# Chunk-selected attention and a SwiGLU layer on one core: two neighbouring query blocks of the selection turned by one transpose

## The chip, the cores and the metric

The kernel runs on one core of a Trainium2 chip. The metric is device time in microseconds (us), the median of several runs. A core has a matrix engine (TensorE, PE in the profile), a vector engine (DVE), a scalar engine (ACT), a general engine (POOL) and a queue engine (SP); each works through its own queue in order, and they meet through semaphores. Matmul results land in PSUM, eight banks of 2 KiB per partition; everything else is in SBUF.

## What is computed

Attention with 4 batches, 8 heads, 768 positions and head size 64, in which each query sees only 6 of 24 chunks of keys, chosen by an upper bound of its scores; then RMS normalisation and a SwiGLU layer (512 to 1536 and back) over the 3072 rows.

```python
k_chunks = k.reshape(B, H, nc, 32, D)
k_min, k_max = np.min(k_chunks, axis=3), np.max(k_chunks, axis=3)
ub = np.sum(np.maximum(q * k_min, q * k_max), axis=-1)      # per query and chunk
ub = np.where(causal, ub, -1e9)
top_chunks = np.argsort(ub, axis=-1)[..., -6:]
scores = scale * q @ k.T, masked to the chosen chunks and to keys not later than the query
attn = softmax(scores) @ v
x = attn rows of all heads side by side
g, val = rmsnorm(x) @ w_gate, rmsnorm(x) @ w_val
out = (silu(g) * val) @ w_out
```

## The kernel before, in words

The work goes by pairs of heads: 16 pairs (4 batches with 4 pairs each). For a pair, `prep` (line 471) loads q and k (SP queue), turns them with TensorE (line 499) so that 128 partitions hold two heads of 64 dimensions, and evicts them to SBUF (`kt`, `qt`). DVE reduces the keys of each chunk to minimum and maximum (lines 523, 525), POOL casts keys and queries to bf16 into the tiles `KE` and `QS` (line 319), and TensorE forms the bounds (line 578, six query groups side by side). The bounds are evicted (`ubs`), turned back so that queries are on partitions (`up`, line 602), and DVE adds the causal term (`ubm`, line 610), takes the eight largest of 24 (`max`, lines 621 to 623, 12 instructions per pair) and writes the selection (`pick`, lines 631 and 636): per query block and head 24 flags and one guard value.

The selection then has to stand on partitions again, beside the queries. `SELQ` holds for each of six query blocks of 128 queries a row of 2 heads x 64 columns, of which 25 are used. `sel_turn` (line 647) turns the six blocks with six transposes of 128x128 into one PSUM tile `st`, 64 partitions per head. `sel_out` (line 655) evicts one half per head into the free half of `QS`: for the first head (hl = 0) queries are in partitions 0 to 63 and flags in 64 to 127, for the second head the other way round. `KE` holds the keys in the same halves, and beside them the indicator rows `e_all`: row c is -30000 in the columns of chunk c, so that one matmul gives score plus mask. `scores` (line 687) runs these matmuls (line 712) over `kk` rows: 89 (64 + 25) for the first head and 128 for the second; for batch 0 a triangular mask is added by a further matmul (line 718), for the others POOL masks after exp (line 735). ACT does exp (line 729), TensorE multiplies by v (line 748), DVE divides (lines 763, 764). `norm` (line 776) and `ffn` (line 844) then work on half batches of 384 rows: 12 tiles of gate and value matmuls (lines 864, 885) with tanh on ACT and two products on DVE (lines 871, 877, 893), and the projection (line 905).

The constants are made at the start: the flags' tile is zeroed by DVE (line 358), `e_all` is built by POOL in four steps (lines 363 to 381) and copied into `KE` by DVE for the first of three buffers and by SP's DMA for the others (lines 387 to 396). `cmf` (line 398) is the causal term.

The order of all instructions is the result of a planner (`Order`, line 107). Each step has engines that it may run on, a cost, dependencies, buffers, and a rank: the sum of entries of two tables, `RANK` (by kind of step, one table for batch 0 and one for the others) and `TIMES` (by place: `a7` is the preparation of pair 7, `l7` its loads, `s7.0` its scores, `n1.0` and `f1.0` normalisation and feed-forward of a half batch, and `step`, `pace...` the increments within a place). The planner simulates the engines with its own costs, takes among the steps that are ready the one of least rank, and emits the instructions in that order. It charges `selC`, the two evictions of the selection, to DVE or ACT, whichever is free, and lets both run at once. The scores of a pair depend on all its `selC` steps in the plan; on the chip an instruction waits only for the tiles that it reads.

Of the kernel before, what the change touches and what calls it, by code (L numbers as in the profile page):

```python
# [8 lines left out]
FP32 = mybir.dt.float32  # L9
BF16 = mybir.dt.bfloat16  # L10
ALU = mybir.AluOpType
ACT = mybir.ActivationFunctionType
# [3 lines left out]
BIGE = 30000.0  # L16
BIGC = 1.0e30
BIGT = -30000.0
THRFLOOR = -5.0e29


GUARD = 480.0
# [5 lines left out]
        av=-17.99, dif=13.38, eps=15.18, exp=27.56, kC=-0.16, kE=17.53, kT=-23.78, kload=11.87,  # L28
        kmn=22.63, kmx=-12.26, max=-61.12, qC=54.11, qE=9.45, qT=-26.18, qload=3.56,
        relu=19.97, root=46.9, sc=-0.2, sel=-44.38, selC=-65.79, selT=-14.62, sq=17.6, tp=7.31,  # L30
        tpE=23.87, ub=-8.14, ubE=18.31, ubm=-7.93, up=-18.76, vload=-10.11, xb=16.97, xs=25.31,
    ),
    dict(
        av=-15.37, dif=-18.4, eps=-17.61, exp=10.72, gate=-5.25, hh=-22.22, kC=13.17, kE=-4.98,
        kT=-1.03, kload=0.17, kmn=-41.84, kmx=7.41, mask=-29.68, max=20.31, out=-9.4, po=2.14,
        poE=-2.1, qC=3.39, qE=-3.84, qT=-9.81, qload=-3.16, relu=-0.35, root=5.16, sc=-14.52,
        sel=-54.35, selC=-24.54, selT=7.81, sq=37.75, tanh=-21.52, tg=-0.17, tp=-45.38,
        tpE=12.9, ub=-13.71, ubE=24.1, ubm=13.82, up=-10.31, val=1.94, vload=19.85, xb=5.4,
        xs=11.14,
# [3 lines left out]
TIMES = dict(  # L43
    pace0=1.79, pace1=0.05, pacen=0.06, step=0.1, w=-2.85, w0=-2.54, w1=11.0, w2=43.12,
    w3=21.59,
)
for p, x in enumerate((
    13.52, 22.61, 22.24, 36.48, 50.85, 112.1, 73.87, -93.04, 37.77, 179.84, 214.26, 206.91,
    226.56, 220.49, 246.48, 309.33,
)):  # L50
    TIMES[f"a{p}"] = x
for p, x in enumerate((
    -126.16, -42.1, -31.16, -25.49, -5.8, -2.4, 25.7, 37.05, 124.03, 155.87, 181.98, 170.69,
    131.44, 202.23, 282.06, 292.24,
)):
    TIMES[f"l{p}"] = x
for p, x in enumerate((
    -21.19, 10.14, 25.24, 47.31, 25.73, 45.99, 41.69, 141.19, 75.77, 129.26, 185.37, 166.25,
    277.81, 251.34, 143.95, 194.34,
)):  # L60
    TIMES[f"s{p}.0"] = x
for p, x in enumerate((
    101.79,
), 3):
    TIMES[f"s{p}.3"] = x
for i, x in enumerate((
    -27.88, 91.19, 93.6, 105.43, 90.44, 106.14, 282.0, 341.37,
)):
    TIMES[f"n{i // 2}.{i % 2}"] = x
for i, x in enumerate((  # L70
    50.8, 120.12, 121.42, 191.74, 229.9, 291.93, 266.48, 339.66,
)):
    TIMES[f"f{i // 2}.{i % 2}"] = x
for i, x in enumerate((
    2.53, 0.58, 0.91, 2.16, 0.75, 2.5, 0.51, 0.73,
)):
    TIMES[f"pacef{i // 2}.{i % 2}"] = x

# [145 lines left out]
def kernel(  # L224
# [23 lines left out]
    HB = NT // 2  # L248
    KM = D + NCH + 1
    W = S // 2  # L250
    G = 3
# [76 lines left out]
    NB = SLOTS["set"]  # L328
# [8 lines left out]
    cmf = const.tile([P, NT, 2, NCH], FP32, name="cmf")  # L337
# [9 lines left out]
    def make_ident(e):  # L347
# [13 lines left out]
        VX[i][:, :, D:D + 1], 1.0)) for i in range(SLOTS["vext"])]  # L361

    def e_step(n):
        if n == 0:
            nc.gpsimd.memset(e_all[:], -BIGE)
        elif n == 1:
            nc.gpsimd.affine_select(
                out=e_all[:], in_=e_all[:], compare_op=ALU.is_ge, fill=0.0,
                base=0, pattern=[[1, S]], channel_multiplier=-CH,
            )  # L370
        elif n == 2:
            nc.gpsimd.affine_select(
                out=e_all[:], in_=e_all[:], compare_op=ALU.is_ge, fill=0.0,
                base=CH - 1, pattern=[[-1, S]], channel_multiplier=CH,
            )
        else:

            nc.gpsimd.affine_select(
                out=e_all[:], in_=e_all[:], compare_op=ALU.not_equal, fill=-1.0,
                base=-NCH, pattern=[[0, S]], channel_multiplier=1,  # L380
            )
# [4 lines left out]
    c_e = prev  # L386
# [11 lines left out]
    def make_cmf(n):  # L398
        if n == 0:
            nc.gpsimd.memset(cmf[:], 0.0)  # L400
        for g4 in (2 * n, 2 * n + 1):
            nc.gpsimd.affine_select(
                out=cmf[32 * g4:32 * (g4 + 1)], in_=cmf[32 * g4:32 * (g4 + 1)],
                compare_op=ALU.is_ge, fill=-BIGC,
                base=g4, pattern=[[4, NT], [0, 2], [-1, NCH]], channel_multiplier=0,
            )

    c_cm = add("cmf", "POOL", 1.5, -70, lambda e: make_cmf(0), [c_e])
# [62 lines left out]
    def prep(c, i0, nb, at, lr):  # L471
# [126 lines left out]
        def up_turn(e):  # L598
            t = tile_of(up, [P, G, nj, 2, CH], FP32, "up")
            for j in range(nj):  # L600
                for h in range(2):
                    nc.tensor.transpose(  # L602
                        t[:, :, j, 1 - h, :], ubs.tile[:, h, j * P:(j + 1) * P],
                        ident_f[0:G * CH, 0:G * CH])
# [3 lines left out]
        def causal(e):  # L608
            t = tile_of(ubm, [P, NT, 2, NCH], FP32, "ubm")
            nc.vector.tensor_tensor(  # L610
                out=t[:, 0:nb].rearrange("p i h c -> p (i h) c"),
                in0=up.tile[:].rearrange("p g j h c -> p (g j h) c")[:, :, 0:NCH],
                in1=cmf[:, i0:i0 + nb].rearrange("p i h c -> p (i h) c"), op=ALU.add)
# [3 lines left out]
        for j in range(0, nb, 3):  # L617
            def top(e, j=j):
                if m8.tile is None:
                    tile_of(m8, [P, NT, 2, 8], FP32, "m8")  # L620
                for x in range(j, j + 3):
                    for h in range(2):
                        nc.vector.max(out=m8.tile[:, x, h, :], in_=ubm.tile[:, x, h, :])

            last = add("max", "DVE", 0.52, rank(at, b, "max", j, "step"), top, [last], opens=[m8], uses=[ubm])
        sq = Buf("selq")

        def pick(e):
            s12 = SELQ[sq.slot][:, 0:nb].rearrange("p i h e -> p (i h) e")
            m12 = m8.tile[:, 0:nb].rearrange("p i h e -> p (i h) e")  # L630
            nc.vector.scalar_tensor_tensor(
                out=s12[:, :, 0:NCH],
                in0=m12[:, :, 5:6].to_broadcast([P, 2 * nb, NCH]),
                scalar=THRFLOOR, in1=ubm.tile[:, 0:nb].rearrange("p i h e -> p (i h) e"),
                op0=ALU.max, op1=ALU.is_gt)
            nc.vector.tensor_scalar(
                out=s12[:, :, NCH:NCH + 1], in0=m12[:, :, 0:1], scalar1=-GUARD,
                scalar2=0.0, op0=ALU.add, op1=ALU.max)
# [5 lines left out]
        def sel_turn(e):  # L644
            t = tile_of(st, [P, nb * P], BF16, "st")
            for j in range(nb):
                nc.tensor.transpose(  # L647
                    t[:, j * P:(j + 1) * P], SELQ[sq.slot][:, j].rearrange("p h c -> p (h c)"),
                    ident_b[:])

        sT = add("selT", "PE", nb * 0.057, rank(at, b, "selT"), sel_turn, [pk, c_idb], opens=[st], uses=[sq])
# [35 lines left out]
    def scores(c, i0, nb, at, pace, adds):  # L687
# [3 lines left out]
        for hl in range(2):  # L691
            kk = slice(0, KM) if hl == 0 else slice(0, P)
# [4 lines left out]
            for g, (nd, regions) in enumerate(groups):  # L697
# [25 lines left out]
                need = list(c.sel) + [y for z in c.ke.values() for y in z] + [c_tri] + c_ke  # L723
# [244 lines left out]
```

## Time and profile before

| | |
|---|---|
| timed runs | 328.67, 330.02, 330.77 us; median 330.02 us |
| profiled execution | span 461.2 us; the profile gives no other time of it |
| granted TensorE clock in it | mean 0.663 |
| busy, share of the span | PE 97%, DVE 53%, ACT 46%, POOL 26% |
| read and written in HBM | 28.57 MB and 6.29 MB |

The profiled execution ran longer than the timed ones, with a lower TensorE clock. How to read it: the page first gives the busy time of each engine; then the span in 40 slices with one digit each for the busy share in tenths (PEclk is the granted TensorE clock in tenths); then the chain of work that ended last, followed back from the last instruction, with its share by engine and line; then groups of instructions: line, engine, operation, output and input tiles with their shapes and the number of instructions, busy us and mean ns of one, and the idle time ahead of them with what ended it. Rows of the timeline give start and length in us, engine, line and operation, and in brackets the idle time before.

### The profile page before, as it was taken

What the parts mean: (1) busy time and instruction counts of PE and PEld (TensorE: products, weight loads), DVE (VectorE), ACT (ScalarE), POOL (GpSimd) and SP (SyncE); (2) the same over time, 40 slices, a digit from 0 to 9 for tenths busy, and PEclk for the clock granted to TensorE, in tenths of its full rate; (3) what the DMA queues carried; (4) which work ended last, traced back from release to release, by engine and by line L of the source; (5) the groups of instructions that cost most, each with busy time, mean ns of one, the idle gap of its engine ahead of it and who ended that gap; (6) DMA issues with size and microseconds to landing.
All of it is one profiled execution on the core that took longest, in us unless ns stands there. A gap on an engine that the chain in (4) does not pass through costs nothing.

```text
span 461.2 us, 7853 instructions
## 1 busy us (share of the span) xinstructions
PE 446.6 (97%) x2978; PEld 253.4 (55%) x2996; DVE 246.5 (53%) x663; ACT 214.3 (46%) x448; POOL 118.0 (26%) x172
## 2 busy tenths in 40 slices
PE   3999999999999999999999999999999999999996
PEld 2677754665666555435666664654565644534442
DVE  2977776665465735404767564367046465603520
ACT  3777772463556643114656684630473634123201
POOL 7755342314442420002552453200110110000000
PEclk9666666666666666666666666666666666666666
DMA  9999769248848250003430203100100000011002
GB/s 186 210 207 143 104 105 100 41 47 53 185 89 134 18 112 9 0 30 105 111 36 1 18 2 46 41 1 1 47 24 0 2 0 1 1 63 52 0 0 91
DMA packets 82645, 27.89 MB, mean 60 GB/s; under 512 B 75568, under 2 KB 79408, under 8 KB 82608
## 3 DMA queue, kind: packets, MB, share of 16 engines
q1 hardware_dynamic: 52528, 19.14, 17.9%
q0 software_dynamic: 28512, 7.87, 17.3%
q10 hardware_dynamic: 1568, 0.39, 0.5%
q8 instruction: 23, 0.38, 0.3%
q14 instruction: 14, 0.11, 0.1%
HBM read 28.57 MB, written 6.29 MB: 76 GB/s over the span
## 4 chain that ended last, share of the span: by engine, by line
PE 96%; DMA 2%; ACT 1%; issue 1%; ACTq 0%
PE vp L885 20%; PE gp L864 20%; PE po L905 20%; PE sc L712 12%; PE av L748 6%; PE ub L578 5%; PE pk L499 3%; PE pq L499 3%; PE tp L830 2%; PE up L602 2%; PE st L647 2%; DMA knat<-in_k_dram 1%; PE sc L718 1%; DMA qnat<-in_q_dram 1%; ACT pt L729 0%
## 5 line engine op out<-in xcount | busy, mean ns | idle before, releaser
L885 PE MATMUL vp<-xT,wv 128*128 128x384 bf16 x384 | 107.5, 430 | 0.0
L864 PE MATMUL gp<-xT,wg 128*128 128x384 bf16 x384 | 107.3, 430 | 0.0
L729 ACT ACTIVATE pt<-sc 128x512 bf16<-128x512 f32 x192 | 91.1, 551 | 20.5 <-PE sc L712 16.6
L905 PE MATMUL po<-wo,hh 128*128 128x512 bf16 x274 | 97.8, 513 | 1.9 <-issue 0.8
L871 ACT ACTIVATE sg<-gp 128x384 bf16<-128x384 f32 x96 | 47.1, 491 | 88.9 <-PE gp L864 78.9
L877 DVE SCALAR_TENSOR_TENSOR tg<-sg,gp 128x384 bf16<-128x384 bf16 x96 | 52.5, 550 | 52.2 <-ACT sg L871 51.4
L893 DVE TENSOR_TENSOR hh<-vp,tg 128x384 bf16<-128x384 f32 x96 | 53.1, 555 | 38.1 <-PE vp L885 37.9
L712 PE MATMUL sc<-qs,ke 89*128 89x128 bf16 (+5 forms) x416 | 72.1, 309 | 0.4 <-PE sc L712 0.2
L885 PEld LDWEIGHTS <-wv 128*128 128x128 bf16 x384 | 45.3, 120 | 43.7 <-issue 3.4
L864 PEld LDWEIGHTS <-wg 128*128 128x128 bf16 x384 | 45.1, 120 | 41.4 <-issue 2.5
L905 PEld LDWEIGHTS <-hh 128*128 128x128 bf16 x288 | 33.5, 120 | 46.8 <-issue 43.8
L735 POOL TENSOR_SCALAR_AFFINE_SELECT pt<-pt 128x512 bf16<-128x512 bf16 (+1 forms) x48 | 24.8, 532 | 102.1 <-ACT pt L729 100.5
L748 PEld LDWEIGHTS <-pt 128*128 128x128 bf16 x672 | 39.1, 111 | 16.5 <-issue 8.2
L712 PEld LDWEIGHTS <-ke 89*128 89x128 bf16 (+1 forms) x420 | 38.2, 116 | 16.0 <-issue 8.6
L748 PE MATMUL av<-vx,pt 128*128 128x65 bf16 x672 | 45.2, 217 | 0.3 <-ACT pt L729 0.2
L317 ACT ACTIVATE osb<-po 128x512 f32<-128x512 f32 x23 | 13.7, 597 | 64.5 <-PE po L905 64.5
L319 POOL CAST ke<-kt 64x768 bf16<-64x768 f32 x31 | 26.1, 843 | 61.0 <-ACT kt L315 57.5
L319 POOL CAST qs<-qt 64x768 bf16<-64x768 f32 x31 | 29.0, 936 | 49.1 <-ACT qt L315 32.5
L499 PE MATMUL pq<-ident_f,qnat 128*128 128x128 f32 x96 | 20.4, 358 | 5.2 <-DMA qnat<-in_q_dram 5.2
L499 PE MATMUL pk<-ident_f,knat 128*128 128x128 f32 x96 | 21.7, 354 | 2.7 <-DMA knat<-in_k_dram 2.5
L525 DVE TENSOR_REDUCE ku<-kt 128x24 f32<-128x768 f32 x16 | 15.1, 945 | 12.7 <-ACT kt L315 12.6
L820 DVE SCALAR_TENSOR_TENSOR xs<-xb,ri,gains 128x512 bf16<-128x512 bf16 x24 | 17.3, 758 | 7.8 <-PE tp L830 5.2
(70 smaller groups left out, 366.7 us busy)
## 6 DMA issues: line engine op xcount, KB each, us to landing
out_dram<-osb SPq DMA_DIRECT2D x24, 256.0 KB, 2.0
qnat<-in_q_dram SPq DMA_DIRECT2D x31, 192.0 KB, 4.8
knat<-in_k_dram SPq DMA_DIRECT2D x31, 192.0 KB, 4.5
vx<-in_v_dram POOLq DMA_DIRECT2D x16, 192.0 KB, 4.7
wv<-in_moe_w_val_dram POOLq DMA_DIRECT2D x2, 768.0 KB, 7.9
wg<-in_moe_w_gate_dram POOLq DMA_DIRECT2D x2, 768.0 KB, 7.0
wo<-in_moe_w_out_dram POOLq DMA_DIRECT2D x2, 768.0 KB, 7.6
ke<-e_all SPq DMA_DIRECT2D x4, 96.0 KB, 3.5
```

Source lines behind the costliest of these rows:

```text
L319: engine[e].tensor_copy(out_, in_)
L499: nc.tensor.transpose(t[:, j * P:(j + 1) * P], nat[w].tile[:, j0 + j].rearrange("p h d -> p (h d)"), ident_f[:])
L712: nc.tensor.matmul(t[:, x:x + m, :].rearrange("p a b -> p (a b)"), ke[kk, kb * P:(kb + 1) * P], qs[kk, q0 * P:(q0 + m) * P], start=not tri ...
L729: nc.scalar.activation(out=t[:, 0:nn, :], in_=sc.tile[:, 0:nn, :], func=ACT.Exp, scale=SCALE)
L735: nc.gpsimd.affine_select(out=pt.tile[:, 0:nd, :], in_=pt.tile[:, 0:nd, :], compare_op=ALU.is_ge, fill=0.0, base=0, pattern=[[0, nd], [1, ...
L748: nc.tensor.matmul(av.tile[:, qi - i0, :], pt.tile[:, x, :], VX[c.v.slot][:, hl * NT + kb, :], start=(begin and m == 0), stop=(left[0] == ...
L864: nc.tensor.matmul(t[:], wg[:, g, hs], XT[b].tile[:, g, cols], start=(g == 0), stop=(g == NP - 1))
L871: nc.scalar.activation(out=t[:], in_=gp.tile[:], func=ACT.Tanh, scale=0.5)
L877: nc.vector.scalar_tensor_tensor(out=t[:], in0=sg.tile[:], scalar=1.0, in1=gp.tile[:], op0=ALU.add, op1=ALU.mult)
L885: nc.tensor.matmul(t[:], wv[:, g, hs], XT[b].tile[:, g, cols], start=(g == 0), stop=(g == NP - 1))
L893: nc.vector.tensor_tensor(out=t[:], in0=vp.tile[:], in1=tg.tile[:], op=ALU.mult)
L905: nc.tensor.matmul(po.tile[:], hhs[ht].tile[:, th * P:(th + 1) * P], wo[:, ht, :], start=(ht == 0), stop=(ht == NHT - 1))
```

## The change

Two neighbouring query blocks (2j and 2j+1) now stand side by side in one row of `SELQ`: 2 heads x 2 blocks x 32 columns, of which 25 are used. One transpose turns both blocks of both heads, three per pair in place of six. In `st` the flags of block 2j lie in the first 32 partitions of a head's half, those of block 2j+1 in the second 32. Four evictions of 32 partitions x 384 columns write them into `QS`, each into every second block of 128 columns; the other 32 partitions of these columns stay zero, from a fill at the start (`qs0`, six fills on DVE). `e_all` stands twice in `KE`'s free half (`e2`, a DVE copy of 32 rows), so that either group of 32 rows meets the indicator rows, and the first head's matmuls take all 128 rows. `e_all` is built on 32 partitions. The order within `ubm`, `m8` and `cmf` follows the pairs of blocks; their sizes stay. All entries of `RANK` and `TIMES` are new; `step` goes from 0.1 to -0.3.

```diff
 TIMES
...
-    pace0=1.79, pace1=0.05, pacen=0.06, step=0.1, w=-2.85, w0=-2.54, w1=11.0, w2=43.12,
...
-    2.53, 0.58, 0.91, 2.16, 0.75, 2.5, 0.51, 0.73,
...
-    TIMES[f"pacef{i // 2}.{i % 2}"] = x
...
+    "l8": 131.77, "l9": 153.75, "n0.0": -62.71, "n0.1": 85.77, "n1.0":
+    -3.47, "n1.1": 171.7, "n2.0": 27.22, "n2.1": 224.25, "n3.0": 361.01, "n3.1": 496.89,
+    "pace0": 0.89, "pace1": 0.41, "pacef0.0": 4.93, "pacef0.1": 2.81, "pacef1.0": 1.95,
+    "pacef1.1": 4.54, "pacef2.0": 3.39, "pacef2.1": 3.3, "pacef3.0": 4.09, "pacef3.1": 2.2,
...
+    "s9.0": 95.26, "step": -0.3, "w": -47.29, "w0": 11.76, "w1": 98.32, "w2": 151.03, "w3":
+    121.51,
...
-    SELQ = [const.tile([P, NT, 2, D], BF16, name=f"selq{i}") for i in range(SLOTS["selq"])]
+    SELQ = [const.tile([P, HB, 2, 2, CH], BF16, name=f"selq{i}") for i in range(SLOTS["selq"])]
...
+    c_qz = []
+    for i in range(NB):
+        for hl, rows in ((0, slice(D, P)), (1, slice(0, D))):
+            c_qz.append(add("qs0", "DVE", 0.38, -85 + 2 * i + hl, lambda e, i=i, hl=hl, rows=rows: nc.vector.memset(
+                QS[i][hl][rows, :], 0.0)))
...
-    c_e = prev
+    c_e = add("e2", "DVE", 0.55, -55, lambda e: nc.vector.tensor_copy(e_all[CH:2 * CH, :], e_all[0:CH, :]),
+              [prev])
...
-            t = tile_of(st, [P, nb * P], BF16, "st")
-            for j in range(nb):
+            t = tile_of(st, [P, W], BF16, "st")
+            for j in range(HB):
                 nc.tensor.transpose(
-                    t[:, j * P:(j + 1) * P], SELQ[sq.slot][:, j].rearrange("p h c -> p (h c)"),
+                    t[:, j * P:(j + 1) * P], SELQ[sq.slot][:, j].rearrange("p h r c -> p (h r c)"),
                     ident_b[:])
...
-        for hl, rows in ((0, slice(D, P)), (1, slice(0, D))):
-            def sel_out(e, hl=hl, rows=rows):
-                evict(e, QS[c.set.slot][hl][rows, cols], st.tile[rows, :])
-
-            fin.append(add("selC", "", {"DVE": dve(n / 2), "ACT": act(n)},
-                           rank(at, b, "selC", hl, "step"), sel_out, [sT],
+        for m, (hl, r) in enumerate(((0, 0), (1, 0), (0, 1), (1, 1))):
+            rows = slice((1 - hl) * D + r * CH, (1 - hl) * D + (r + 1) * CH)
+
+            def sel_out(e, hl=hl, r=r, rows=rows):
+                evict(e, QS[c.set.slot][hl][rows, :].rearrange("p (j r n) -> p j r n", r=2, n=P)[:, :, r, :],
+                      st.tile[rows, :].rearrange("p (j n) -> p j n", n=P))
+
+            fin.append(add("selC", "", {"DVE": dve(W / 2), "ACT": act(W)},
+                           rank(at, b, "selC", m, "step"), sel_out, [sT],
                            opens=[c.set], uses=[st]))
...
-            kk = slice(0, KM) if hl == 0 else slice(0, P)
+            kk = slice(0, P)
...
-                need = list(c.sel) + [y for z in c.ke.values() for y in z] + [c_tri] + c_ke
+                need = list(c.sel) + [y for z in c.ke.values() for y in z] + [c_tri] + c_ke + c_qz
```

More of the change, by code (lines that the diff above doesn't have):

```diff
@@ L27 @@
     dict(
[L28 to L31, printed above, removed]
+        av=-42.22, dif=67.0, eps=-14.19, exp=69.47, kC=62.54, kE=135.16, kT=-129.54,
+        kload=12.44, kmn=104.45, kmx=216.29, max=-56.99, qC=114.05, qE=30.74, qT=-22.31,
@@ L32 @@
+        qload=-14.31, relu=1.45, root=50.83, sc=-37.2, sel=-55.79, selC=-86.89, selT=-91.77,
+        sq=45.31, tp=96.79, tpE=82.56, ub=143.96, ubE=-178.44, ubm=-72.0, up=-27.24,
+        vload=-57.02, xb=45.55, xs=-2.48,
     ),
     dict(
-        av=-15.37, dif=-18.4, eps=-17.61, exp=10.72, gate=-5.25, hh=-22.22, kC=13.17, kE=-4.98,
-        kT=-1.03, kload=0.17, kmn=-41.84, kmx=7.41, mask=-29.68, max=20.31, out=-9.4, po=2.14,
-        poE=-2.1, qC=3.39, qE=-3.84, qT=-9.81, qload=-3.16, relu=-0.35, root=5.16, sc=-14.52,
@@ L52 @@
[L52 to L74, printed above, removed]
-    2.53, 0.58, 0.91, 2.16, 0.75, 2.5, 0.51, 0.73,
-)):
-    TIMES[f"pacef{i // 2}.{i % 2}"] = x
+        av=0.26, dif=4.16, eps=-130.07, exp=33.84, gate=13.12, hh=-55.72, kC=-3.18, kE=-141.97,
+        kT=6.78, kload=44.27, kmn=-146.74, kmx=35.69, mask=-107.0, max=-2.66, out=-43.19,
+        po=28.39, poE=-34.42, qC=84.36, qE=1.98, qT=3.31, qload=39.11, relu=18.41, root=193.12,
@@ L85 @@
+        sc=-12.75, sel=-284.46, selC=-70.59, selT=30.64, sq=-75.76, tanh=-52.95, tg=-107.28,
+        tp=-2.25, tpE=66.99, ub=58.81, ubE=75.42, ubm=226.55, up=-103.71, val=20.43,
+        vload=46.21, xb=-52.04, xs=-181.25,
+    ),
+)
+TIMES = {
[15 rows of a table added]
+}
 class Buf:
@@ L248 @@
     HB = NT // 2
-    KM = D + NCH + 1
     W = S // 2
@@ L361 @@
         VX[i][:, :, D:D + 1], 1.0)) for i in range(SLOTS["vext"])]
+    c_qz = []
[3 more added lines that the diff above has]
+                QS[i][hl][rows, :], 0.0)))
     def e_step(n):
         if n == 0:
-            nc.gpsimd.memset(e_all[:], -BIGE)
+            nc.gpsimd.memset(e_all[0:CH], -BIGE)
         elif n == 1:
             nc.gpsimd.affine_select(
-                out=e_all[:], in_=e_all[:], compare_op=ALU.is_ge, fill=0.0,
+                out=e_all[0:CH], in_=e_all[0:CH], compare_op=ALU.is_ge, fill=0.0,
                 base=0, pattern=[[1, S]], channel_multiplier=-CH,
@@ L372, in e_step @@
             nc.gpsimd.affine_select(
-                out=e_all[:], in_=e_all[:], compare_op=ALU.is_ge, fill=0.0,
+                out=e_all[0:CH], in_=e_all[0:CH], compare_op=ALU.is_ge, fill=0.0,
                 base=CH - 1, pattern=[[-1, S]], channel_multiplier=CH,
@@ L378, in e_step @@
             nc.gpsimd.affine_select(
-                out=e_all[:], in_=e_all[:], compare_op=ALU.not_equal, fill=-1.0,
+                out=e_all[0:CH], in_=e_all[0:CH], compare_op=ALU.not_equal, fill=-1.0,
                 base=-NCH, pattern=[[0, S]], channel_multiplier=1,
@@ L404, in make_cmf @@
                 compare_op=ALU.is_ge, fill=-BIGC,
-                base=g4, pattern=[[4, NT], [0, 2], [-1, NCH]], channel_multiplier=0,
+                base=g4, pattern=[[8, HB], [0, 2], [4, 2], [-1, NCH]], channel_multiplier=0,
             )
-    c_cm = add("cmf", "POOL", 1.5, -70, lambda e: make_cmf(0), [c_e])
+    c_cm = add("cmf", "POOL", 1.5, -70, lambda e: make_cmf(0), [prev])
     c_cm = add("cmf", "POOL", 1.1, -69, lambda e: make_cmf(1), [c_cm])
@@ L602, in up_turn @@
                     nc.tensor.transpose(
-                        t[:, :, j, 1 - h, :], ubs.tile[:, h, j * P:(j + 1) * P],
+                        t[:, :, 1 - h, j, :], ubs.tile[:, h, j * P:(j + 1) * P],
                         ident_f[0:G * CH, 0:G * CH])
@@ L608, in causal @@
         def causal(e):
[L609 removed]
+            t = tile_of(ubm, [P, 2 * NT, NCH], FP32, "ubm")
             nc.vector.tensor_tensor(
[L611 to L613 removed]
+                out=t[:], in0=up.tile[:].rearrange("p g h j c -> p (g h j) c")[:, :, 0:NCH],
+                in1=cmf[:].rearrange("p g h j c -> p (g h j) c"), op=ALU.add)
         last = add("ubm", "DVE", 0.07 + nb * 48 * 0.00104, rank(at, b, "ubm"), causal, [ut, c_cm],
@@ L619, in top @@
                 if m8.tile is None:
[L620 to L623, printed above, removed]
+                    tile_of(m8, [P, 2 * NT, 8], FP32, "m8")
+                for x in range(2 * j, 2 * j + 6):
+                    nc.vector.max(out=m8.tile[:, x, :], in_=ubm.tile[:, x, :])
             last = add("max", "DVE", 0.52, rank(at, b, "max", j, "step"), top, [last], opens=[m8], uses=[ubm])
```

27 lines of the change are left out of this document (7 added, 20 removed), and 10 rows, old and new, of the table TIMES.

## The prediction

> **What bounds the kernel now.** I read the page first (busy time, slices, chain), then the busy time by stretch, then the chain of waits by line, then the timeline around the selection.
>
> ```profile
> span 461.2 us, 7853 instructions
> ...
> PE 446.6 (97%) x2978; PEld 253.4 (55%) x2996; DVE 246.5 (53%) x663; ACT 214.3 (46%) x448; POOL 118.0 (26%) x172
> ...
> PEclk9666666666666666666666666666666666666666
> ...
> PE 96%; DMA 2%; ACT 1%; issue 1%; ACTq 0%
> ```
>
> In the profiled execution TensorE (PE) is busy almost without a break and the chain that ended last runs 96% through it, at a granted clock near two thirds. The profile gives no other time of that execution than its span of 461.2 us; the median of the timed runs, 330.02 us, is 0.716 of it. So the timed runs had a faster PE than this trace, and a stretch that PE bounds here may be bound by something else there. The stretches tell how far:
>
> ```profile
> 0.00:11.50 11.50, 3.74 (x17) 3.38 (x18) 3.26 (x11) 4.42 (x8) 8.14 (x24) 1.00 1.05 186
> ...
> 449.70:461.20 11.50, 7.66 (x24) 2.62 (x22) 0.00 (x0) 1.65 (x3) 0.00 (x0) 0.64 0.24 91
> ```
>
> ```profile
> 11.50:65.00 53.50, 53.10 (x585) 37.49 (x584) 42.98 (x141) 40.39 (x89) 27.85 (x35) 0.66 1.08 165
> 65.00:170.00 105.00, 104.00 (x734) 61.34 (x740) 63.90 (x174) 52.19 (x109) 36.16 (x47) 0.65 0.59 80
> ...
> sum 449.70, PE 442.81 PEld 250.07 DVE 243.28 ACT 209.92 POOL 109.91; mean PE 73.80 PEld 41.68 DVE 40.55 ACT 34.99 POOL 18.32
> ```
>
> The columns are the stretch, its length, then PE, PEld, DVE, ACT, POOL busy, the clock, DMA. After the first 11.5 us PE works 442.81 us at 0.65. At full clock that is 288 us, with the first 3.74 us 291.6 us. A timed run of 330.0 us therefore has a clock between 288/318.5 = 0.90 (PE never idle after 11.5 us) and 1.00 (then 38.4 us idle). At such a clock the attention-only stretch of 11.5 to 65 us needs 35 to 38 us of PE, but 42.98 us of DVE: there DVE bounds. Later PE does, for the most part (104.00 us become 68 to 75, DVE 63.90).
>
> **The change part by part.**
>
> *Transposes.* Six per pair of heads become three; 16 pairs, 48 removed.
>
> ```profile
> L647 PE MATMUL st<-ident_b,selq 128*128 128x128 bf16 x96 | 10.6, 263 | 0.0
> ```
>
> ```profile
> by line: PE vp L885 20.4%; PE gp L864 20.3%; PE po L905 19.9%; PE sc L712 11.6%; PE av L748 6.1%; PE ub L578 4.9%; PE pk L499 3.5%; PE pq L499 3.0%; PE tp L830 1.7%; PE up L602 1.7%; PE st L647 1.6%; DMA knat<-in_k_dram 1.0%; PE sc L718 0.9
> ```
>
> ```profile
> 11.50:65.00 53.50, 3.18 (x30) 2.79 (x5) 4.02 (x5) 0.66 1.08 165
> ...
> 280.00:365.00 85.00, 2.04 (x18) 1.66 (x3) 2.42 (x3) 0.65 0.05 20
> ```
>
> (The last two rows are of the selection's PSUM tile alone: PE, DVE, ACT.) The 263 ns include the pipeline. On the chain the 96 hold 1.6% of 461.2 us = 7.4 us, 77 ns each (10.6/96 = 110 ns is the upper bound, with overlap). 48 x 77 ns = 3.7 us; their weight loads lie beside PE. Nothing is late next: PE goes on with whatever stands behind. Against the span: 461.2 - 3.7 = 457.5 us. In timed runs, by 0.716, -2.65 us; between -3.8 (110 ns) and -1.7 (of the 30 in the DVE-bound stretch 15 go and gain nothing there; 33 x 77 ns x 0.65). The Trainium skill (TensorE: Matmul & The Clock Gate, Back-to-back issue gap) gives about 81 ns for a load and matmul of 128 columns at full clock; an estimate from it is 48 x 81 ns = 3.9 us, and the time would be 326.1 us. The trace has 77 ns at 0.65 of the clock, so I stay with the row.
>
> *Wider scores.* The first head contracts over 128 rows, not 89.
>
> ```profile
> L712 PE MATMUL sc<-qs,ke 128*128 128x128 bf16 x162 | 22.7, 262 | 0.0
> L712 PE MATMUL sc<-qs,ke 89*128 89x128 bf16 x162 | 22.0, 266 | 0.0
> ...
> L712 PE MATMUL sc<-qs,ke 89*128 89x512 bf16 x30 | 13.2, 506 | 0.0
> ...
> L712 PE MATMUL sc<-qs,ke 128*128 128x512 bf16 x26 | 11.4, 494 | 0.0
> ```
>
> Both widths stand there and last alike: 0 (between -12 and +4 ns each).
>
> *Evictions.* Two copies of 64x768 per pair become four of 32x384, 256 bytes apart in the target. All read one PSUM tile.
>
> ```profile
> L315 ACT ACTIVATE qt<-pq 128x384 f32<-128x384 f32 x27 | 13.0, 489 | 16.1 <-PE pq L499 15.9
> L315 ACT ACTIVATE qs<-st 64x768 bf16<-64x768 bf16 x16 | 12.9, 806 | 11.4 <-PE st L647 7.3 <-DVE qs L319 4.0
> ...
> L319 DVE COPY qs<-st 64x768 bf16<-64x768 bf16 x16 | 8.9, 553 | 20.1 <-ACT qs L315 13.0 <-PE st L647 7.0
> ...
> L319 DVE COPY xT<-tp 128x512 bf16<-128x512 bf16 x5 | 2.1, 425 | 4.3 <-PE tp L830 4.2
> ```
>
> ACT has 384 columns at 489 ns. On DVE 256 elements lie between 425 and 553 ns, 0.5 ns each, so 384 cost about 0.36 us (not above the 553). Two on each engine: ACT 0.98 for 0.81 us, DVE 0.72 for 0.55: +0.17 us on each engine and pair, 2.7 us each in all, beside PE. In the DVE-bound stretch five pairs hold 0.85 us of DVE; between 0 and +0.85 us of the time, and I leave it in the range. More weighs the latency:
>
> ```profile
> 353.55 0.70 PE L647 MATMUL st<-ident_b,selq 128*128 128x128 bf16 x6
> ```
>
> ```profile
> 354.33 0.81 ACT L315 ACTIVATE qs<-st 64x768 bf16<-64x768 bf16 x1
> ```
>
> ```profile
> 355.17 0.55 DVE L319 COPY qs<-st 64x768 bf16<-64x768 bf16 x1 [1.80 <-ACT qs L315]
> ```
>
> ```profile
> 356.02 1.46 PE L712 MATMUL sc<-qs,ke 89*128 89x128 bf16 x10
> ```
>
> ```profile
> DVE qs L319 <- ACT qs L315: 13.0, 11, 2.8
> ...
> ACT qs L315 <- DVE qs L319: 4.0, 5, 1.6
> ```
>
> The two evictions never overlap, though the planner charges them in parallel: DVE waits for ACT (11 times) or ACT for DVE (5 times), 16 of 16. The Trainium skill (PSUM — Partial Sum Buffer, PSUM bank collisions raise a hardware error) lets two engines read one bank at the same time in different quadrants; in this trace the two read different halves, and still in turn, 0.03 us apart. If they did go two at a time, the four would take about 0.95 us, the cover would hold, and 327.4 us would stand. Four in turn last 0.08 + 2 x 0.49 + 2 x 0.36 + 3 x 0.03 = 1.87 us from the last transpose; before, the first head's scores waited only for the first copy, 0.89 us. In the new ranks the step has the sign that puts the first head's first copy last (step -0.3 for +0.1), so its scores wait for all four. What covers them is PE's other work between transpose and score, 1.77 us here, 1.15 to 1.28 us at the timed clock, and by the planner's own charge (two ACT copies of 384 for one of 768) 0.07 us more. In the profiled execution the cover holds within 0.03 us; at the timed clock 0.5 to 0.65 us per pair are open. PE takes its queue in order, so every matmul behind that score waits too, and exp on ACT behind it. Bounds: 0 to 16 x 0.65 = +10.4 us. I take 0, nearest to the rows, which show no PE wait at a score, and make the rest a rival.
>
> *The start.* Six zero fills of 64x768 and one copy of 32x768 are new on DVE, the three fills of the selection tiles halve.
>
> ```profile
> 2.07 0.38 DVE L358 MEMSET selq<- 128x384 uint32 x1
> ...
> 5.33 0.51 DVE L391 COPY ke<-e_all 64x768 bf16<-64x768 bf16 x1 [2.88 <-POOL e_all L378]
> ...
> 5.85 0.56 DVE L392 COPY ke<-e_all 64x768 bf16<-64x768 bf16 x1
> ...
> 7.29 0.56 DVE L560 TENSOR_SCALAR rt<-qt 128x768 f32<-128x768 f32 x1 [0.87 <-ACT qt L315]
> ...
> 8.69 0.83 SPq L395 DMA_DIRECT2D ke<-e_all  x1
> ```
>
> 6 x 0.38 - 3 x 0.19 = 1.7 us fit into DVE's 2.88 us of idle time; the copy (0.5 us) takes most of the 0.87 us ahead of L560. The key copies on SP start at 8.69 us, 2 us later than their source would then be ready, so SP's queue does not move. Cost 0; without that cover up to 0.5 us on the start. Bounds and top-8 instructions keep count and size; DMAs are the same.
>
> *The order.* Every rank is new. Feed-forward steps are spread wider (pace 1.95 to 4.93 for 0.51 to 2.53), and in eight pairs (4, 5, 6, 8, 9, 10, 14, 15) the scores' rank lies below that of their transpose, so they go as soon as they can. The trace of before cannot price it: PE's 38.4 us of idle time at full clock, less 7.8 at the start, 3.8 at the end and 8 where DVE bounds, leave at most 19 us to win; as much to lose. Nearest are the rows of the profiled execution, where PE has next to no gap: 0.
>
> **Sum.** 461.2 - 3.7 + 0 + 0 + 0 = 457.5 us profiled; timed 330.02 - 2.65 = **327.4 us**.
>
> **The rivals.** *Late evictions (slower).* At the timed clock the scores come 0.58 us late; where they follow at once, in 8 to 13 of 16 pairs, that is 4.6 to 7.5 us: 332 to 335 us. It decides from about 0.3 us in each pair (2.65/8). For it: 16 of 16 in turn, the sign of the step, eight pairs ranked for at once. Against it: PE already idles at a timed clock near 1.00, and part of the delay may fall into idle time.
>
> *A better order (faster).* The wider spread of the feed-forward puts PE work between attention steps bound by DVE; a third of the 19 us returns, 6.2 us: 321.2 us. For it: DVE's 42.98 us beside 35 to 38 of PE early on; against it: that stretch has no feed-forward work yet.
>
> *A worse order (slower).* One batch's normalisation comes later and PE runs dry once, 10 us: 338 us. Little speaks for it.
>
> *Nothing moves.* If timed runs wait on DVE and ACT in every attention stretch, the 48 transposes fall into idle time: 330 us, within the first case's own range.
>
> **How the numbers follow.** Saving arrives, 327.4 us (own range 324 to 330.5): 0.36. Late evictions: 0.32. Better order: 0.25. Worse order: 0.07. About 1% is what a measurement can tell, so the limits are 326.7 and 333.3 us. Faster: 0.14 of the first, 0.24 of the third, 0.38. Within: 0.22, 0.05 of the second, 0.01, 0.28. Slower: 0.27 and 0.07, 0.34. The range reaches from 318 (half a better order more) to 337 us, with about one in ten outside on each side.
>
> **What would show it.** The selection transposes x48 at 1.6% / 2 of the chain; scores all at 128 rows with the same mean; four evictions in turn over about 1.8 us; the fills done before 5.3 us. A PE wait at the scores for the eviction of the selection shows the late rival, less DVE idle time in the second stretch the better order. If the profiled span falls by other than 3 to 4 us, the order did it; if the span falls and the time does not, the timed clock hides what PE saves.

## The result and the profile after

The changed kernel takes 333.12 us, the one before 329.35 us: a ratio of 1.013, with a 95% interval of 1.0092 to 1.0167. It is slower by 1.3%, where 0.8% faster was forecast (2.65 of 330.02 us); the time lies in the range, and in the place of the rival with the late evictions (332 to 335 us). In all runs of this case the kernel before takes 328.3 to 329.4 us at a granted clock of 0.997 or more and 329.7 to 330.8 us at 0.994 or 0.995, so two medians are alike only as far as their clocks are.

The profile of the changed kernel was taken at full TensorE clock, the one of before at 0.65 after its start. To compare like with like, the kernel before was profiled once more (the first run below), now at 1.00 too: a span of 326.8 us for 331.4. First the busy times, the changed kernel and then the kernel before at this clock:

```profile
span 331.4 us, 7841 instructions
...
PE 309.9 (93%) x2948; PEld 198.3 (60%) x2948; DVE 246.1 (74%) x684; ACT 209.2 (63%) x464; POOL 120.9 (36%) x174
...
PE 76%; DVE 12%; ACT 7%; DMA 2%; issue 2%; ACTq 0%; DVEq 0%
```

```profile
span 326.8 us, 7871 instructions
...
PE 311.1 (95%) x2996; PEld 200.5 (61%) x2996; DVE 242.1 (74%) x663; ACT 206.1 (63%) x448; POOL 119.2 (36%) x172
...
PE 87%; DVE 4%; ACT 4%; DMA 2%; issue 1%; POOL 1%; ACTq 0%; POOLq 0%
```

PE works 1.2 us less and idles 5.8 us more (21.5 for 15.7 us): together the 4.6 us of span. The chain that ended last now runs 12% through DVE and 7% through ACT, for 4% each. What the added steps wait for stands in the waits of PE, changed kernel first:

```profile
PE sc L694 <- DVE qs L296: 4.0, 6, 1.2
...
PE sc L694 <- ACT qs L292: 2.2, 3, 0.9
```

```profile
PE sc L712 <- ACT qs L315: 0.2, 1, 0.2
```

Each of these rows gives who waited for whom, the us in all, the number of waits and the longest. The scores (L694, formerly L712) wait 6.2 us in nine places for the evictions of the selection, where they waited 0.2 us. One of these places, in the timelines of PE, DVE and ACT, shows how it comes about:

```profile
43.31 0.33 PE L626 MATMUL st<-ident_b,selq 128*128 128x128 bf16 x3
...
44.07 0.35 DVE L296 COPY qs<-st 32x384 bf16<-32x384 bf16 x1
...
44.46 0.48 ACT L292 ACTIVATE qs<-st 32x384 bf16<-32x384 bf16 x1 [0.22 <-DVE qs L296]
...
44.97 0.71 DVE L296 COPY qs<-st 32x384 bf16<-32x384 bf16 x2 [0.55 <-ACT qs L292]
...
45.74 0.38 PE L694 MATMUL sc<-qs,ke 128*128 128x128 bf16 x4 [1.16 <-DVE qs L296]
```

The transposes end at 43.64 us. Four copies (here three on DVE and one on ACT) follow one after the other, from 44.07 to 45.68 us, and the first head's scores start with the end of the last. By engine (groups of the changed kernel, then of the one before):

```profile
L292 ACT ACTIVATE qs<-st 32x384 bf16<-32x384 bf16 x32 | 15.4, 482 | 10.2 <-DVE qs L296 8.0 <-PE st L626 2.0
...
L296 DVE COPY qs<-st 32x384 bf16<-32x384 bf16 x32 | 11.3, 352 | 9.0 <-ACT qs L292 8.3 <-PE st L626 0.4
...
L626 PE MATMUL st<-ident_b,selq 128*128 128x128 bf16 x48 | 5.3, 220 | 0.7 <-DVE qt L296 0.6
```

```profile
L712 PE MATMUL sc<-qs,ke 128*128 128x128 bf16 x162 | 17.9, 219 | 0.3 <-DVE xb L764 0.3
...
L712 PE MATMUL sc<-qs,ke 89*128 89x128 bf16 x162 | 16.7, 218 | 0.3 <-ACT qs L315 0.2
...
L315 ACT ACTIVATE qs<-st 64x768 bf16<-64x768 bf16 x16 | 12.9, 805 | 6.4 <-PE st L647 3.7 <-DVE qs L319 2.5
...
L319 DVE COPY qs<-st 64x768 bf16<-64x768 bf16 x16 | 8.8, 553 | 8.6 <-ACT qs L315 6.8 <-PE st L647 1.7
...
L647 PE MATMUL st<-ident_b,selq 128*128 128x128 bf16 x96 | 8.0, 219 | 1.4 <-DVE selq L636 1.1 <-ACT pt L729 0.2
```

The transposes save 8.0 - 5.3 = 2.7 us of PE, as forecast. The copies take 26.7 us of ACT and DVE for 21.7, and the idle time ahead of them rises from 15.0 to 19.2 us, of which 16.3 us is one engine waiting for the other's copy (9.3 us before).

Where the loss falls, in two rows of the stretches of each (stretch, length, then PE, PEld, DVE, ACT, POOL busy); the changed kernel, then before:

```profile
11.50:60.00 48.50, 41.19 (x564) 29.15 (x564) 42.67 (x155) 39.78 (x92) 29.10 (x37) 1.00 1.37 199
...
120.00:170.00 50.00, 48.63 (x449) 30.36 (x449) 43.20 (x128) 35.12 (x83) 17.56 (x27) 1.00 0.44 75
```

```profile
11.50:60.00 48.50, 44.79 (x608) 31.52 (x607) 45.88 (x149) 41.58 (x96) 29.79 (x38) 1.00 1.16 182
...
120.00:170.00 50.00, 50.00 (x364) 30.53 (x362) 32.87 (x72) 26.96 (x58) 15.14 (x19) 1.00 0.37 88
```

3.6 us of PE are lost up to 60 us, for the most part in the attention of the first batch, and 1.4 us between 120 and 170 us. In the first of these stretches PE has next to no feed-forward work to do meanwhile: the gate and value matmuls hold 1.4 us of PE there.

### The profile page after: what moved, and what is told of

It reads as the page before. It is cut to its first block, busy times and chain, and to the rows that moved or that the text cites. A ratio compares the mean times of both kernels' runs of the same rounds, so it can differ in the third digit from the quotient of the medians.

```text
span 331.4 us, 7841 instructions
## 1 busy us (share of the span) xinstructions
PE 309.9 (93%) x2948; PEld 198.3 (60%) x2948; DVE 246.1 (74%) x684; ACT 209.2 (63%) x464; POOL 120.9 (36%) x174
## 4 chain that ended last, share of the span: by engine, by line
PE 76%; DVE 12%; ACT 7%; DMA 2%; issue 2%; ACTq 0%; DVEq 0%
PE po L887 18%; PE vp L867 16%; PE gp L846 16%; PE sc L694 9%; PE av L730 4%; PE ub L561 4%; ACT qs L292 4%; DVE qs L296 3%; PE pk L482 3%; PE pq L482 2%; PE up L585 2%; PE tp L812 1%; DVE m L604 1%; ACT pt L711 1%; DMA knat<-in_k_dram 1%
## 5 line engine op out<-in xcount | busy, mean ns | idle before, releaser
L867 PE MATMUL vp<-xT,wv 128*128 128x384 bf16 x384 | 76.7, 326 | 0.1
L846 PE MATMUL gp<-xT,wg 128*128 128x384 bf16 x384 | 76.5, 326 | 0.0
L887 PE MATMUL po<-wo,hh 128*128 128x512 bf16 x288 | 68.3, 379 | 0.0
L694 PE MATMUL sc<-qs,ke 128*128 128x128 bf16 (+2 forms) x420 | 54.9, 251 | 6.6 <-DVE qs L296 4.0
L846 PEld LDWEIGHTS <-wg 128*128 128x128 bf16 x384 | 36.6, 98 | 23.4 <-issue 0.4
L867 PEld LDWEIGHTS <-wv 128*128 128x128 bf16 x384 | 36.2, 98 | 23.9 <-issue 1.9
L694 PEld LDWEIGHTS <-ke 128*128 128x128 bf16 x420 | 30.4, 97 | 17.3 <-issue 8.6
L730 PE MATMUL av<-vx,pt 128*128 128x65 bf16 x672 | 37.3, 194 | 1.3 <-ACT pt L711 1.0
L730 PEld LDWEIGHTS <-pt 128*128 128x128 bf16 x672 | 31.2, 98 | 11.6 <-ACT pt L711 3.6
L296 POOL CAST qs<-qt 64x768 bf16<-64x768 f32 x31 | 27.6, 891 | 21.5 <-ACT qt L292 13.6
L292 ACT ACTIVATE qs<-st 32x384 bf16<-32x384 bf16 x32 | 15.4, 482 | 10.2 <-DVE qs L296 8.0
```

Source lines behind the costliest of these rows:

```text
L292: nc.scalar.activation(out=out_, in_=in_, func=ACT.Copy)
L296: engine[e].tensor_copy(out_, in_)
L694: nc.tensor.matmul(t[:, x:x + m, :].rearrange("p a b -> p (a b)"), ke[kk, kb * P:(kb + 1) * P], qs[kk, q0 * P:(q0 + m) * P], start=not tri ...
L730: nc.tensor.matmul(av.tile[:, qi - i0, :], pt.tile[:, x, :], VX[c.v.slot][:, hl * NT + kb, :], start=(begin and m == 0), stop=(left[0] == ...
L846: nc.tensor.matmul(t[:], wg[:, g, hs], XT[b].tile[:, g, cols], start=(g == 0), stop=(g == NP - 1))
L867: nc.tensor.matmul(t[:], wv[:, g, hs], XT[b].tile[:, g, cols], start=(g == 0), stop=(g == NP - 1))
```

## The experiments

Two theories stood at the start. **Late evictions**: four copies in turn last longer than PE's cover, and the plan does not know it. **The order**: the new ranks are worse on the chip, and the copies only show it. A third, more work on DVE and ACT, was carried along. Each ratio is to runs of the kernel before on the same chip, 328.5 to 328.7 us except where said.

**The kernel before, profiled at full clock.** No edit.

> The kernel before, unchanged, for a profile at the clock of the changed kernel's profile (1.00, span 331.4 us). Expected: span near 327 us; its first-head scores follow the first copy of the selection by 0.1 us or more without a PE wait if late evictions explain the loss (PE waits at the scores below 1 us in all, against 6.2 us in the changed kernel); if the order explains it, the PE waits at the scores are alike in both and the difference stands at other lines.

328.49 us, span 326.8 us, PE waits at the scores 0.5 us in all. This is the reference for the section above, and the waits speak for the late evictions.

**First head first.** The first head's two copies come ahead of the second's.

```diff
-        for m, (hl, r) in enumerate(((0, 0), (1, 0), (0, 1), (1, 1))):
+        for m, (hl, r) in enumerate(((1, 1), (1, 0), (0, 1), (0, 0))):
```

> The changed kernel with one line changed: the four evictions come in the order that gives the first head both of its copies first, then the second head's. The plan and the order of every other instruction stay. Late evictions: of the 6.2 us that PE waits at scores for the selection most goes (the two copies that are waited for end 0.85 us earlier), 328 to 330 us for 333.1. New order of the ranks: 333 us, no change. More work on DVE and ACT: 333 us, no change.

331.64 us, ratio to before 1.0074 (1.0047 to 1.0101). The waits of the scores for the copies fall from 6.2 to 1.4 us, as expected, but the time by 1.5 us only, less than the 3 to 5 us expected of late evictions. So the wait at the first score is not the whole cost: in its place PE now waits 0.9 us ahead of the bounds for DVE and 0.7 us for the division (`xb`).

```profile
PE sc L694 <- ACT qs L292: 1.1, 2, 0.8
...
PE ub L561 <- DVE ku L517: 0.9, 1, 0.9
...
PE sc L694 <- DVE xb L746: 0.7, 1, 0.7
...
PE sc L694 <- DVE qs L296: 0.3, 1, 0.3
```

**Half of the evictions.**

```diff
-                evict(e, QS[c.set.slot][hl][rows, :].rearrange(...)[:, :, r, :],
+                if r == 0: evict(e, QS[c.set.slot][hl][rows, :].rearrange(...)[:, :, r, :],
```

> The changed kernel without the two evictions of the second block of each pair of blocks (so the flags of every second query block are left out of the result); plan and order of all else stay. Late evictions: two copies in turn last 0.87 us as before the change, PE waits at scores near 0, 326 to 328 us. More work on DVE and ACT alone: 2 copies x 16 pairs are 7.7 us of ACT or 5.6 us of DVE less, 331 to 332 us. Order: 333 us.

326.04 us, 0.9893 (0.9852 to 0.9934), at a granted clock of 0.993 in all four runs. The loss is gone, with ranks and order unchanged: the copies carry it.

**Each transpose twice.**

```diff
-            for j in range(HB):
+            for j in [0, 0, 1, 1, 2, 2]:
```

> The changed kernel with each of the three transposes issued twice in a row, 48 more in all, at the planned places. If PE bounds: 48 x 54 to 77 ns = 2.6 to 3.7 us more, 335.7 to 336.8 us for 333.1. If the transposes lie in time that PE idles anyway: 333.1 to 334 us.

333.96 us, 1.015 (1.0111 to 1.0189): 0.8 us more than the changed kernel, for 2.7 us of PE work. Most of it falls into time that PE idles.

**All copies on DVE; one engine per head.** Both with the first head first.

```diff
-                evict(e, QS[c.set.slot][hl][rows, :].rearrange(...)[:, :, r, :],
+                evict("DVE", QS[c.set.slot][hl][rows, :].rearrange(...)[:, :, r, :],
```

```diff
-                evict(e, QS[c.set.slot][hl][rows, :].rearrange(...)[:, :, r, :],
+                evict("DVE" if hl == 0 else "ACT", QS[c.set.slot][hl][rows, :].rearrange(...)[:, :, r, :],
```

> The first-head-first version with all four evictions issued on DVE (plan and PE order as before). DVE gets 32 x 0.35 = 11.3 us more work, ACT 15.4 us less, and neither waits for the other within the four (17 us of such waits go). Late scores alone: the first head is ready 0.15 us earlier than with alternating engines, 331 us. The two queues held by alternating copies: 328 to 330 us. More work on DVE: 335 us or more.

> The first-head-first version with the first head's two evictions on DVE and then the second head's two on ACT: the same work as with alternating engines, but one hand-over per pair of heads instead of up to three. Late scores alone: 331 us. The two queues held by alternating copies: 329 to 330 us. More work on DVE and ACT: 331.6 us, no change.

335.17 us (1.0206, 1.0188 to 1.0224) and 336.87 us (1.0255, 1.0239 to 1.027). Both lose against the alternating copies, 331.64 us. The hand-overs as the cost are not borne out. But both also give an engine work where the plan had counted on the other, so they do not settle it. The first shows that the length of the turn is not all: four copies in a row on DVE last 1.5 us, less than four by turns, and yet the time rises by 3.5 us, with DVE busy for 258.3 us in place of 245.7.

**The ranks exchanged.** The new code with the old tables, the old code with the new ones.

> The changed code with the ranks of before (they were not searched for it; the step of 0.1 gives the copies in the order first head, second head, first head, second head). If the new ranks are the loss: 328 to 330 us. If the copies are the loss: 332 us or more, with PE waits at scores for the selection again.

> The code before with the new ranks (not searched for it). If the new ranks are the loss: 332 us or more. If the copies are the loss and the ranks are as good: 327 to 330 us.

342.34 us (1.041, 1.0393 to 1.0428) and 339.2 us (1.0322, 1.0307 to 1.0338). Both are far slower than either kernel, so neither table is the better one: each fits its own code, and the other's table costs the new code 9.2 us and the old one 10.6 us, in runs whose clock was 0.985 to 0.995. As a test of the order it is a miss: the first run meets what was expected of the copies, the second what was expected of the ranks.

**Two wide copies.** The new code and ranks, with two copies of the size of before, the first head's first. The selection itself is left out by a further line that is not shown.

```diff
-                evict(e, QS[c.set.slot][hl][rows, :].rearrange(...)[:, :, r, :],
-                      st.tile[rows, :].rearrange("p (j n) -> p j n", n=P))
+                if r == 0: evict(e, QS[c.set.slot][hl][(1 - hl) * D:(2 - hl) * D, :].rearrange("p (r j) -> p r j", r=2),
+                      st.tile[(1 - hl) * D:(2 - hl) * D, :].rearrange("p (r j) -> p r j", r=1).to_broadcast([D, 2, W]))
```

> The changed kernel with two copies of 64x768 per pair of heads, as before the change, in place of four of 32x384, first head first; three transposes, new ranks and plan stay. (So that the flags do no harm in the wrong block, the selection itself is left out: the comparison gives zero for every chunk and every causal key is used; sizes and instructions are the same.) If the four copies are the loss: 327 to 328.5 us, the time before less what the transposes save. If the new order loses by itself: 331 to 333 us.

325.88 us, 0.9903 (0.9872 to 0.9934). So all of the change but its four copies is worth 2.8 us. The two copies also stand on one engine in ten of the 16 pairs, and the waits of one engine for the other's copy are 2.0 us in all. Its first stretch:

```profile
11.50:60.00 48.50, 44.57 (x593) 31.03 (x592) 43.95 (x157) 41.83 (x96) 30.65 (x39) 1.00 1.36 203
```

PE has its 44.57 us there again, for 41.19 in the changed kernel: the new order is not at fault.

**Four copies in the kernel before.** The first head's last copy comes last, as in the changed kernel, and the engines take turns whatever the plan says.

```diff
-                evict(e, QS[c.set.slot][hl][rows, cols], st.tile[rows, :])
+                o = {"ACT": "DVE", "DVE": "ACT"}[e]
+                for x, y in ((1, e if hl == 0 else o), (0, o if hl == 0 else e)):
+                    evict(y, QS[c.set.slot][x][(1 - x) * D:(2 - x) * D, (1 - hl) * W:(2 - hl) * W], st.tile[(1 - x) * D:(2 - x) * D, (1 - hl) * W:(2 - hl) * W])
```

> The kernel before, ranks and plan kept, with its two evictions per pair split into four of 64x384 that go to the two engines by turns, the first head's last copy last. If the four copies are the loss: 333 us or a little more (the changed kernel less its saved transposes). If the new order is: 328.7 to 330 us.

337.77 us, 1.0245 (1.0196 to 1.0294), 9.1 us more. Four copies in this order, put into the old kernel with its old ranks, make more than the whole loss, with the same waits of PE:

```profile
PE sc L714 <- DVE qs L319: 5.1, 9, 1.2
...
PE sc L714 <- ACT qs L315: 2.7, 3, 1.2
```

**The copies charged as they run.** In both codes the planner is told that the copies follow each other, and new ranks are searched for each against the planner's own span. By the old charges that span was 319.8 us before the change and 319.0 us after it: by the plan the change gained.

```diff
+        last = sT
+        for hl in range(2):
...
+            last = add("selC", "", {"DVE": 0.74, "ACT": 1.0},
+                       rank(at, b, "selC", hl, "step"), sel_out, [sT, last],
```

```diff
-            fin.append(add("selC", "", {"DVE": dve(n / 2), "ACT": act(n)},
-                           rank(at, b, "selC", hl, "step"), sel_out, [sT],
+            fin.append(add("selC", "", {"DVE": 0.57, "ACT": 0.82},
+                           rank(at, b, "selC", hl, "step"), sel_out, [sT] + fin,
```

> The changed code with the copies charged in the plan as they run: two steps per pair, each with both copies of one head on one engine (0.74 us on DVE, 1.00 on ACT), the second step after the first; ranks searched anew for it against the planner's own span. If the loss of the change is that the plan does not know of the copies' turns: 327 us or less. If the four copies hold the engines whatever the plan knows: 331 us or more.

> The code before with its two copies charged as they run (0.57 us on DVE, 0.82 on ACT, the second after the first), ranks searched in the same way. If a plan that knows the turns gains by itself: 325 to 327 us. If not: 328 to 331 us. Beside the run above it tells what the three transposes with four copies are worth when both plans know what they do.

The new code: 328.09 us, 0.997 (0.9952 to 0.9988), 5.0 us less than with the old charges. The old code: 325.08 us, 0.9887 (0.9849 to 0.9925), 3.5 us less than with the old charges and faster than both kernels. The loss of the change shrinks but stays: at a granted clock of 0.997 or more the new code was 4.6 us behind the old one with the old charges (333.1 and 328.5 us) and is 2.0 us behind with the new ones (327.1 and 325.1 us; 3.0 us by the medians, as six of the new code's ten runs had 0.992 to 0.995). So the four copies do not cost 7 us under every plan. The old code meets what was expected of a plan that knows the turns; the new code meets neither expectation. How much of each gain comes from the charges and how much from a further search is not shown: no search with the old charges was repeated beside it.

**Four copies in two places.** In place of forced engines: the first head's two copies in the plan's first place, the second head's in another, each on the planned engine.

```diff
-                evict(e, QS[c.set.slot][hl][rows, :].rearrange(...)[:, :, r, :],
+                for x in range(2 if r == 0 else 0):
+                    rows = slice((1 - hl) * D + x * CH, (1 - hl) * D + (x + 1) * CH)
+                    evict(e, QS[c.set.slot][hl][rows, :].rearrange(...)[:, :, x, :],
```

> The changed kernel with all four copies, but issued as in the version with two wide copies: in two of the four planned places, each with both copies of one head on the engine that the plan had given that place (first head first). Against the four alternating copies with the first head first (331.6 us) the work and the first head's readiness stay and the hand-overs between the engines drop; against the two wide copies (325.9 us) the places stay and only 0.17 us per engine and pair of work is added. If the hand-overs hold the engines: 326 to 328 us. If four copies cost whatever their turns: 330 us or more.

332.49 us, 1.011 (1.0087 to 1.0133). The waits between the engines fall from 16.0 to 3.1 us, and the time does not: the hand-overs are not the cost. The waits with the first head first, and here:

```profile
ACT qs L292 <- DVE qs L296: 8.1, 17, 0.9
DVE qs L296 <- ACT qs L292: 7.9, 15, 0.7
```

```profile
ACT qs L292 <- DVE qs L296: 2.4, 2, 1.5
...
DVE qs L296 <- ACT qs L292: 0.7, 1, 0.7
```

**Four short copies.** By turns, the first head first.

```diff
-                evict(e, QS[c.set.slot][hl][rows, :].rearrange("p (j r n) -> p j r n", r=2, n=P)[:, :, r, :],
-                      st.tile[rows, :].rearrange("p (j n) -> p j n", n=P))
+                evict(e, QS[c.set.slot][hl][rows, :].rearrange("p (j r n) -> p j r n", r=2, n=P)[:, :, r, 0:CH],
+                      st.tile[rows, :].rearrange("p (j n) -> p j n", n=P)[:, :, 0:CH])
```

> The version with four alternating copies, first head first (331.6 us), with each copy cut from 384 to 96 columns (the flags of three quarters of the queries are left out): the four copies, their places, engines and hand-overs stay, only their length goes, from 0.48 and 0.35 us to about 0.25 and 0.22 us, and the four in turn from 1.8 to about 1.0 us, less than two wide copies take. If the length of the four in turn is the cost: 325.5 to 327 us. If the number of copies or hand-overs is: 330 us or more.

325.02 us, with 329.87 us for the kernel before on that chip, 0.9865 (0.9837 to 0.9893); the runs of before at a clock of 0.998 or more took 328.6 to 329.2 us. Number, places and hand-overs of the copies are those of the first-head-first version, and the loss is gone. Their lengths:

```profile
L292 ACT ACTIVATE qs<-st 32x96 bf16<-32x96 bf16 x32 | 7.7, 241 | 7.1 <-DVE qs L296 4.5 <-PE st L626 2.0
...
L296 DVE COPY qs<-st 32x96 bf16<-32x96 bf16 x32 | 6.5, 202 | 4.6 <-ACT qs L292 3.6 <-PE st L626 0.4
```

Four in turn come to 2 x 0.24 + 2 x 0.20 = 0.89 us and the gaps. So it is the length of the copies that costs, not their number, their places or their hand-overs. From the first copy's start to the last one's end a pair takes, as a median of the timelines, 1.76 us with the first head first and 1.76 us in two places (331.6 and 332.5 us of time), 1.39 us with two wide copies (325.9 us) and 0.99 us with four short ones (325.0 us).

What an early start of the first head does not cure is 5.8 of the 7.2 us between the changed kernel and the one with two wide copies. The second head's later flags and the later exits of both engines to their next work are left for it; how these share it stays open, since a shorter copy both shortens the turn and takes work from the engines. The step from four copies to two wide ones takes 5.4 us of copying from the two engines and gives 5.8 us. The step from two wide to half of the evictions takes another 8.4 us and gives 1 to 2 us at like clocks (327.59 us in the one run at 0.992, 325.6 to 326.5 us at 0.993). So engine work alone, at one price per us, does not explain both.

**Two wide copies, each transpose twice.** The edits of these two versions together.

> The version with two wide copies (325.9 us, selection left out as there) with each transpose issued twice: 48 more. If the transposes count in full once the copies do not hold PE: 328.5 us (2.6 us more). If they count as little as in the changed kernel with six transposes (0.8 us): 326.7 us.

327.52 us, 0.9951 (0.9931 to 0.9972): 1.6 us more than with three transposes. Where the copies do not hold PE, 48 transposes are worth 1.6 of their 2.7 us.

## Why the prediction was wrong

**The step that failed** is the latency of the evictions, put at 0 as "nearest to the rows, which show no PE wait at a score". Those rows came from an execution at 0.65 of the clock, and the cover in them was read at one pair, at 354 us, where it lasted 1.77 us. The same text had the cover at 1.15 to 1.28 us at the timed clock, shorter than its 1.87 us of copies, and left that to a rival. The changed kernel was not profiled at 0.65, so what it would have waited there is not shown. Measured: at full clock PE waits 6.2 us at the scores for the selection, and the price of the four copies is 7.2 us here (333.12 less 325.88) and 9.1 us in the kernel before, inside the bounds of 0 to 10.4 and near their upper end. With it the sum would have been 327.4 + 7.2 = 334.6 us.

The rest of the sum came out in total, 2.8 us of gain for 2.65, but by luck: the transposes gave less than forecast, and something that was put at 0 gave the remainder.

**The rival** named the wait, the sign of the step and the price (4.6 to 7.5 us). Its mechanism is right but too narrow: it priced the first head's wait. Turning the order round gives back 1.5 us, shortening the four 6.6 us more. Its places are right in part only: the eight pairs that it named are of the second batch and later, and 2.9 of the 6.2 us stand at scores of the first batch, at 21.20, 38.69 and 45.74 us, which the triangular mask's matmul (L700) follows.

```profile
21.20 0.38 PE L694 MATMUL sc<-qs,ke 128*128 128x128 bf16 x4 [0.85 <-ACT qs L292]
...
38.69 0.38 PE L694 MATMUL sc<-qs,ke 128*128 128x128 bf16 x4 [0.90 <-DVE qs L296]
```

**The transposes.** 2.7 us of PE work, right. Of the time 0.8 us in the changed kernel and 1.6 us where the copies do not hold, for the 2.65 us of the sum: nearest to the lower bound of 1.7 us, which left out the transposes of the stretch that it held to be bound by DVE. The 81 ns of the Trainium skill (TensorE: Matmul & The Clock Gate, Back-to-back issue gap) are not borne out: (8.0 - 5.3)/48 = 56 ns at full clock.

**Wider scores.** Right: at full clock 218 ns for 89 rows and 219 ns for 128 in the kernel before, and 219 ns for all 324 in the changed one.

**Work on the engines.** 0.49 and 0.36 us forecast for 384 columns, 0.48 and 0.35 measured.

**The start.** The fills ended before the copies needed DVE, as DVE's timeline of the changed kernel shows:

```profile
2.31 2.86 DVE L342 MEMSET qs<- 64x384 uint32 x6
5.32 0.51 DVE L368 COPY e_all<-e_all 32x768 bf16<-32x768 bf16 x1
```

The six fills took 2.86 us, more than the 6 x 0.38 us of the working, and still fitted. PE's wait for the first keys grew from 2.5 to 3.0 us all the same, also in the version with two wide copies, so it does not come from the copies; what else makes it was not tried.

**The order.** Taken at 0. With two wide copies all else is worth 2.8 us, of which 1.6 us are the transposes: some 1.1 us are left for the order and whatever else changed, within its bounds. No run has the order alone.

**The clock.** Between 0.90 and 1.00 forecast; 1.00 in three of the four timed runs and 0.988 in one. The idle time at full clock was overstated, 38.4 us for 15.7: PE's busy time went to 0.70 (446.6 to 311.1 us), not to 0.65. The kernel before at 0.65, then at 1.00:

```profile
L905 PE MATMUL po<-wo,hh 128*128 128x512 bf16 x274 | 97.8, 513 | 1.9 <-issue 0.8
```

```profile
L905 PE MATMUL po<-wo,hh 128*128 128x512 bf16 x288 | 68.5, 379 | 0.0
```

With the scores of 128 columns (262 and 219 ns) that is 0.65 and 0.42 ns per column, and 178 and 166 ns that do not go by the columns. So a part of each matmul's recorded time hardly shrank.

## What to carry to other kernels

When the profile was taken at another clock than the timed runs, price each cover at the timed clock: a wait that PE's slow work hides in the trace can appear in the time. A plan that charges two readers of one PSUM tile in parallel is blind to every further reader; here true charges and a new search together gave the old code 3.5 us without any other change (which of the two gave it was not separated). Halving the transposes is not a saving if the same data then leave PSUM in twice as many pieces.

## What the runs showed of the hardware

One and the same kernel was profiled with a span of 461.2 us at 0.65 of the TensorE clock and of 326.8 us at 1.00; DVE's 242 to 247 us and ACT's 206 to 214 us were nearly the same in both.

A bf16 copy out of PSUM cost by its columns, and the same for 32 as for 64 partitions: 64x384 took 484 ns on ACT and 356 ns on DVE (four copies in the kernel before), 32x384 took 482 and 352 ns, 32x96 took 241 and 202 ns. From 96 to 384 columns that is 0.84 and 0.52 ns per column, and some 0.16 and 0.15 us for each copy beside. These figures give 0.80 and 0.55 us for 64x768; 805 and 553 ns were measured.
